# FNet mixing and a squared-ReLU layer on one core: the first tile's table on ScalarE's queue, and P's products ahead of Q's in the first front

## The chip, the core and the metric

The kernel runs on one core of a Trainium2 chip. The metric is the device time in microseconds (us) of one execution; less is better. Before the change the median of three runs is 1860.83 us, and the three lie between 1860.78 and 1861.01. One execution was also profiled; it took 1860.65 us, and its span, from the first instruction to the last, is 1858.6 us. The other 2.05 us lie outside the span.

The core's engines each work through their own instructions in order: TensorE (PE) multiplies matrices, VectorE (DVE), ScalarE (ACT) and GpSimd (POOL) work elementwise, SyncE (SP) issues most transfers. An engine that meets an instruction whose semaphores are not yet there stops until they are. Transfers that SP issues run on one queue (q1 in the profile), those that ACT issues on another (q10), those of POOL on a third (q0).

## What is computed

```python
def _attn_ref(x):                       # x: (8, 3008, 256)
    X = np.fft.fft(x, axis=1)
    X = np.fft.fft(X, axis=2)
    return X.real.astype(np.float32)

def _moe_ref(x, w_in, w_out):           # x: (24064, 256), w_in: (256, 2048), w_out: (2048, 256)
    h = x @ w_in
    r = np.maximum(h, 0.0)
    g = r * r
    return (g @ w_out).astype(np.float32)
```

The real part of a two-dimensional Fourier transform of each of 8 batches, then a two-layer network with a squared ReLU on each of the 24064 rows. x is float32. The weights arrive as 64-bit floats; the kernel loads them as pairs of 32-bit words and makes float32 of them itself.

## The kernel before

**The whole.** The transform along the sequence is made by products with cosine and sine tables, after the 3008 rows have been folded by their symmetries into 7 tiles. For each batch this gives two panels, Pt (cosine part, called P) and Qt (sine part, called Q), each of 128 features by 1505 frequencies. The transform along the features is multiplied into w_in once: G1 and G2 are w_in times a cosine and a sine table. Then h is G1 with Pt plus or minus G2 with Qt, and from h the network goes on. A "front" is one step of this, for a block of 252 frequencies and a pair of chunks of 128 hidden features: products with P, products with Q, then DVE adds and subtracts them into g. Each batch has 6 blocks of 8 fronts. After a front come ReLU and square on ACT, sums on POOL, and the products with w_out in a bilinear scheme with few multiplications (lines 1063 to 1125).

**The head.** In the first 31 us, batch 0's tiles are loaded, folded and multiplied while the tables and the first raw weights arrive. This part is written out by hand from line 1320 on. The tiles are 0 and 1 (95 and 94 rows), TWO = 2 and TWO + 1 = 3 (96 and 92 rows), and ODD0 = 4, 5 and 6 (128, 128 and 120 rows). They are worked off in the order 0, 4, 1, 5, 2, 3, 6. For each:

- `load_x` issues one transfer for x, on SP's queue; `load_table` issues the transfers for the cosine table, one for each run of rows that lies together (three for tile 0, one for tile 4), on the queue it is given, SP's by default;
- `fold` adds and subtracts rows on DVE; its last result w goes to the products; two columns of w go to `lone` by ACT (line 577);
- `turn_table` makes the sine table from the cosine table on ACT (line 228). Tile 0's sine table is loaded instead, on POOL's queue;
- `products_of("P0 E0")` and the like put the products on PE (line 769): P with the cosine table, Q with the sine table, E with the cosine table and the single column.

`awake(n)` (line 252) puts n products of the identity matrix with itself on PE. Their results are never read. Before tile 0's products there are 24 of them, after them 7.

`round_win(j, raw)` gives the steps by which the raw 64-bit words of chunk pair j of w_in become float32. In the hand-written part these are `first` (pair 0) and `second` (pair 1): `[0]` begins on DVE (line 300), `[1]` is two steps on ACT (lines 305 and 310), `[2]` is on DVE (line 320), `[3]` is the sum on POOL (line 329). `first[0]` stands on DVE between the folds of tiles 1 and 5.

`join_4`, `join_2` and `lo` put together parts of Pt and Qt on DVE (lines 817 to 823, 811 to 813); "lo" writes the 252 columns that the first front needs. `keep` copies the odd part out of its PSUM bank on ACT (line 830). For P that bank belongs to the pool `psh`, which has two buffers; the fronts of the head take theirs from the same pool. `ends_of(0)` multiplies G2 with a single column on PE (line 383), and `keep_ends` copies its two columns into gE on DVE (line 387); DVE needs gE and the window ew when it splits a front (line 1026).

**The order after the head.** `ORDER` (line 1446) is a list of tokens, each of which issues a step to one engine. Those that matter here: `sp` multiplies to spread one row of Qt over all partitions (PE, line 995), `et` copies the result into the window ew (ACT, line 996); `f0a` and `f0b` are the products of the two halves of front 0 (PE, lines 1011 and 1013), `d0a` and `d0b` split them on DVE (lines 1026 to 1029); `TSj`, `Hj` are the DVE steps of weight pair j (lines 300, 320), `PUj`, `PLj`, `PWj` its ACT steps, `PRj` its POOL step; `pgDj`, `pgCj` multiply it with the sine and the cosine table (PE, line 351), `GDj`, `GCj` copy these into G2 and G1 (ACT, line 374).

**Semaphores of transfers.** The transfers that SP and ACT issue take their semaphores in turn from the same eight, in the order in which the transfers are placed in the program. A transfer that takes a semaphore for the second time waits, before it is issued, until the transfer that had it before has landed.

Of the kernel before, what the change touches and what calls it, by code (L numbers as in the profile page):

```python
# [9 lines left out]
F32 = mybir.dt.float32  # L10
# [5 lines left out]
P = 128  # L16
# [68 lines left out]
def kernel(  # L85
# [12 lines left out]
    nc = tc.nc  # L98
# [8 lines left out]
    CH = 256  # L107
# [13 lines left out]
    fp = ctx.enter_context(tc.tile_pool(name="fp", bufs=3))  # L121
# [4 lines left out]
    sp = ctx.enter_context(tc.tile_pool(name="sp", bufs=2))  # L126
# [5 lines left out]
    psh = ctx.enter_context(tc.tile_pool(name="psh", bufs=2, space=PSUM))  # L132
# [13 lines left out]
    TWO = ODD0 - 2  # L146
# [14 lines left out]
    def later_rows(t):  # L161

        if t >= ODD0:
            return [(p, S // 8 + 1 + first, count, 1) for p, first, count in ODD[t - ODD0]]
        c, r0, step, rows = TILES[t]
        if t == TWO + 1:
            return [(p, TILES[TWO][1] + step * (2 * HALF2 - p - R), R, step) for p in range(0, ROWS2, R)]
        return [(0, r0, rows, step)]

    def load_x(b, t):  # L170
        if b and (t >= ODD0 or t == TWO + 1):
            xt[b, t] = xp.tile([P, 4, D], F32, name="xt", tag="x")
            for p, first, count, step in later_rows(t):
                nc.sync.dma_start(out=xt[b, t][p:p + count], in_=x[b, first:first + step * (count - 1) + 1:step])
            return
        c, r0, step, rows = TILES[t]

        while rows % 15 and rows % 16 and r0 + step * rows < NROW:
            rows += 1

        pool, tag = (gp, "g") if b == 0 and t < NT - NX else (xp, "x")
        xt[b, t] = pool.tile([P, 4, D], F32, name="xt", tag=tag)
        nc.sync.dma_start(out=xt[b, t][0:rows], in_=x[b, r0:r0 + step * (rows - 1) + 1:step])
# [4 lines left out]
    def load_later(i):  # L188
        if i < len(LATER):
            load_x(*LATER[i])  # L190
# [3 lines left out]
    cosT, sinT = ([const.tile([P, 2, WT], F32, name=nm), sp.tile([P, 2, WL], F32, name=nm + "l", tag="s")]  # L194
                  for nm in ("cosT", "sinT"))

    def part_of(tab, t):
        return tab[t in LATE]
# [4 lines left out]
    G1 = const.tile([P, F], F32, name="G1")  # L203
# [4 lines left out]
    def load_table(tab, src, tiles, queue=nc.sync):  # L208

        for t in tiles:  # L210
            c, r0, step, rows = TILES[t]
            for i, (s0, count) in enumerate(row_tiles(S)):
                mine = [r for r in range(count) if (s0 + r - r0) % step == 0 and 0 <= (s0 + r - r0) // step < rows]
                if mine:
                    o, m = (s0 + mine[0] - r0) // step, len(mine)
                    while m % 15 and m % 16 and o + m < P and mine[0] + step * m < P:
                        m += 1
                    nk = NC[0][c]
                    queue.dma_start(out=part_of(tab, t)[o:o + m, :, PLACE[t]:PLACE[t] + nk],
                                    in_=src[mine[0]:mine[0] + step * (m - 1) + 1:step, :, i, 0:nk])  # L220
# [31 lines left out]
    def awake(n):  # L252
        filled = psh.tile([P, CH], F32, name="filled", tag="h")
        for _ in range(n):
            nc.tensor.matmul(filled[:, 0:P], ident, ident, start=True, stop=True)
# [123 lines left out]
    def ends_of(j):  # L379
        ps = psd.tile([P, CH], F32, name="pe", tag="d")  # L380
        for h in range(2):
            fc = j + NJ * h
            nc.tensor.matmul(ps[:, h:h + 1], G2[:, fc * P:(fc + 1) * P], last, start=True, stop=True)
        return ps

    def keep_ends(j, ps):
        nc.vector.tensor_copy(gE[:, j::NJ], ps[:, 0:2])

    def take_ends(j):
        nc.sync.dma_start(out=gE[:, j::NJ], in_=g_dram[j].rearrange("(h f) -> f h", h=2))  # L390
# [612 lines left out]
    def store_upper():  # L1003
        nc.sync.dma_start(out=e_dram[0:1, KH:NKT], in_=PQE[0][1][P - 1:P, KH:NKT])

    def front_half(b, k0, n, j, h):

        pt, qt = PQE[b]
        ks, fs = slice(k0, k0 + n), slice((j + NJ * h) * P, (j + NJ * h + 1) * P)
        ps = psh.tile([P, 2, CH], F32, name="ph", tag="h")  # L1010
        nc.tensor.matmul(ps[:, 0, 0:n], G1[:, fs], pt[:, ks], start=True, stop=True)
        rows = P if b else P - 1
        nc.tensor.matmul(ps[:, 1, 0:n], G2[0:rows, fs], qt[0:rows, ks], start=True, stop=True)  # L1013
        return ps
# [291 lines left out]
    def p_part(*names):  # L1306
        for nm in names:
            for kp in range(2):
                groups[0, kp, nm]()

    def q_part(*names):
        for nm in names:
            for kp in range(2):
                groups[1, kp, nm]()
# [3 lines left out]
            (p_part if nm[0] == "P" else q_part)({"P": "", "Q": "", "E": "e"}[nm[0]] + nm[1:])  # L1318

    start()  # L1320
    awake(24)
    load_x(0, 0)
    load_table(cosT, cos_s, (0,))
    load_x(0, ODD0)
    load_x(0, 1)
    nc.scalar.copy(turn[0:1, 0, 0:1], ident[0:1, 0:1])
    nc.gpsimd.tensor_copy(turn[0:1, 0, 1:2], xt[0, 0][0:1, 0, 0:1])
    load_table(sinT, sin_s, (0,), nc.gpsimd)
    load_table(cosT, cos_s, (1, TWO, TWO + 1), nc.gpsimd)
    load_table(cosT, cos_s, (ODD0,))  # L1330
    load_x(0, ODD0 + 1)
    raw = {("in", 0): load(pair_in(0))}
# [2 lines left out]
    for dst, src in ((cosd, cos_d), (sind[:, :, 0:P - 1], sin_d)):  # L1335
        nc.sync.dma_start(out=dst, in_=src.rearrange("(c p) m -> p c m", p=P))
    load_x(0, TWO + 1)
    load_x(0, ODD0 + 2)
    load_table(cosT, cos_s, (ODD0 + 2,))
    first = round_win(0, raw["in", 0])  # L1340
# [34 lines left out]
    sc = fold(ODD0 + 2, 1)  # L1375
    fold_beside(ODD0 + 2, sc)
    products_of("P6 E6")
    ends = ends_of(0)
    p_part("join_2")
    q_part("join_4")  # L1380
    products_of("Q6")
    second = round_win(1, raw["in", 1])
    second[0]()
    second[1]()
    p_part("lo", "keep")
    q_part("join_2")
    keep_ends(0, ends)
    q_part("lo")
    BLOCKS = [(k0, min(CK, NKT + 1 - k0)) for k0 in range(0, NKT, CK)]
    assert all(n % 3 == 0 for _, n in BLOCKS)  # L1390
    steps = [(b, k0, n, j) for b in range(B) for k0, n in BLOCKS for j in range(NJ)]
# [44 lines left out]
    def piece_beside():  # L1436
# [7 lines left out]
    ROUNDED = ['3', 'w0', '4', 'w1', '5', 'w2', '6', 'w3', '7', 'w4', 'w5', 'w6', 'w7']  # L1444
    PHASES = ('TS', 'PW', 'H', 'PR', 'PU', 'PL')
    ORDER = (
        'sp H1 PR1 TS2 PU2 TS3 f0a et PL2 f0b PW3 d0a H2 PR2 pgD1 d0b pgC1 GD1 TSw0 GC1 lc4 H3 PR3 rl0 PWw0 fe1 f1b gE1 pgC2 f1a '
        'd1b pgD2 GC2 d1a GD2 keep f2b TS4 fe2 rl1 pgD3 Hw0 gE2 GD3 dE3 pgC3 sq0 PRw0 d2b f2a GC3 TSw1 PW4 d2a f3b sq1 '
        'PWw1 H4 bk0 PR4 TS5 Hw1 rl2 PRw1 PW5 pgD4 f3a GD4 dE4 d3b pgC4 TSw2 d3a sq2 bk1 GC4 H5 PWw2 PR5 TS6 Hw2 '
        'PW6 PRw2 rl3 TSw3 H6 PWw3 pgD5 PR6 f4b GD5 dE5 f4a d4b sq3 pgC5 d4a bk2 GC5 rl4 TS7 Hw3 PW7 PRw3 TSw4 H7 lc1 '  # L1450
# [56 lines left out]
    def step(token):  # L1507


        what, nm = re.fullmatch("([A-Za-z]+?)(w?[0-9]*[ab]?)", token).groups()  # L1510
        if what in PHASES:
            rounds[nm][PHASES.index(what)]()
            if what == "H":
                freed.add(nm)
                load_more()
        elif what == "sp":
            made["et"] = spread_e()
        elif what == "et":
            made["et"]()
        elif what == "df":  # L1520
            for f in beginning:
                f()
        elif what == "lc":
            load_columns(int(nm or 4))
        elif what == "xl":
            for k in range(NX):
                load_later(k)
        elif what == "keep":
            q_part("keep")
        elif what == "restQ":  # L1530
            q_part("rest")
        elif what == "restP":
            p_part("rest")
        elif what == "spl":
            store_lower()
            load_window(0, *BLOCKS[1])
        elif what in ("pgC", "pgD"):
            made[what, nm] = dft_win(int(nm), int(what == "pgD"))
        elif what in ("GC", "GD"):
            keep_win(int(nm), int(what == "GD"), made["pg" + what[1], nm])  # L1540
        elif what == "fe":
            made["fe", nm] = ends_of(int(nm))
        elif what == "gE":
            keep_ends(int(nm), made["fe", nm])
        elif what == "dE":
            take_ends(int(nm))
        elif what in "fd":
            i, h = int(nm[:-1]), int(nm[-1] == "b")
            if what == "f":
                if i >= NJ and ("x", i) not in made:  # L1550
                    made["x", i] = True
                    load_columns(4)
                made[token] = front_half(*steps[i], h)
            else:
                split_half(*steps[i], h, front_at(i)[-1], made["f" + nm])
        elif what in ("rl", "sq"):
            (relu if what == "rl" else square)(steps[int(nm)][2], made["g", int(nm)])
        elif what == "cm":
            sums_of(int(nm))
        elif what in ("sc", "su"):  # L1560
            (copy_wout if what == "sc" else sum_wout)(int(nm[0]), int(nm[1] == "b"))
        elif what == "hi":
            rows_at(int(nm))
        else:
            assert what == "bk"
            back_at(int(nm))
# [20 lines left out]
    for i in range(PLAIN, len(steps) + 2):  # L1587
        if i < len(steps):
            b, k0, n, j = steps[i]
# [130 lines left out]
```

## Time and profile before

| | |
|---|---|
| median of three runs | 1860.83 us (1860.78 to 1861.01) |
| the profiled execution | 1860.65 us |
| its span | 1858.6 us |
| PE, idle in the first 100 us | 2.58 us |
| DVE, busy from 15 to 30 us | 14.83 of 15 us |
| the 16 DMA engines, busy from 5 to 30 us | 1.01 to 1.10 of each 5 us, as the profile counts it |

In a row of the timeline the first number is the start and the second the duration, both in us from the span's start; then come engine, line, operation, what is written and read, shapes and how many instructions the row stands for. In square brackets stands how long the engine had been idle and who ended it. PE shows two records for one float32 product. A row of the stages view gives a stretch, its length and for each engine the busy time and the number of instructions; PEclk is the share of the TensorE clock that was granted, and the last two numbers are the share of the DMA engines and GB/s.

### The profile page before, as it was taken

What the parts mean: (1) busy time and instruction counts of PE and PEld (TensorE: products, weight loads), DVE (VectorE), ACT (ScalarE), POOL (GpSimd) and SP (SyncE); (2) the same over time, 40 slices, a digit from 0 to 9 for tenths busy, and PEclk for the clock granted to TensorE, in tenths of its full rate; (3) what the DMA queues carried; (4) which work ended last, traced back from release to release, by engine and by line L of the source; (5) the groups of instructions that cost most, each with busy time, mean ns of one, the idle gap of its engine ahead of it and who ended that gap; (6) DMA issues with size and microseconds to landing.
All of it is one profiled execution on the core that took longest, in us unless ns stands there. A gap on an engine that the chain in (4) does not pass through costs nothing.

```text
span 1858.6 us, 33954 instructions
## 1 busy us (share of the span) xinstructions
PE 1850.1 (100%) x11360; PEld 1748.1 (94%) x11360; DVE 1474.3 (79%) x3472; ACT 1075.2 (58%) x1594; POOL 1461.2 (79%) x2137
## 2 busy tenths in 40 slices
PE   9999999999999999999999999999999999999999
PEld 7699999999999999999999999999999999999998
DVE  8998878887788878778788787788878887757666
ACT  5776546565555655656456564565645666444454
POOL 4499778788788887888778887788877878787885
PEclk9999999999999999999999999999999999999999
DMA  7441101111111101111011100111001100000010
GB/s 211 109 61 41 21 21 51 41 29 23 29 34 45 26 22 32 33 46 30 15 32 46 49 15 15 46 46 35 15 21 44 37 15 21 17 21 15 21 43 23
DMA packets 153265, 69.51 MB, mean 37 GB/s; under 512 B 132577, under 2 KB 144325, under 8 KB 153092
## 3 DMA queue, kind: packets, MB, share of 16 engines
q1 hardware_dynamic: 152546, 66.80, 14.6%
q8 instruction: 91, 1.49, 0.3%
q14 instruction: 82, 0.67, 0.1%
q0 software_dynamic: 416, 0.43, 0.1%
q10 hardware_dynamic: 130, 0.12, 0.0%
HBM read 42.60 MB, written 24.69 MB: 36 GB/s over the span
## 4 chain that ended last, share of the span: by engine, by line
PE 94%; DVE 2%; POOL 1%; ACT 1%; issue 0%; DMA 0%; SPq 0%; POOLq 0%; DVEq 0%; ACTq 0%
PE F L1105 34%; PE S L1105 23%; PE hQ L1040 17%; PE hP L1040 17%; PE pd L893 1%; PE pd L867 1%; PE pd L769 1%; PE pg L351 0%; PE fin L1214 0%; DVE fd L320 0%; DVE he L1026 0%; DVE wsum L420 0%; DVE g L1029 0%; ACT g L1053 0%; PE ph L1013 0%
## 5 line engine op out<-in xcount | busy, mean ns | idle before, releaser
L1053 ACT ACTIVATE g<-g 128x1008 f32<-128x1008 f32 (+1 forms) x384 | 399.4, 1040 | 307.3 <-DVE g L1049 282.1
L1044 DVE SCALAR_TENSOR_TENSOR he<-ew,gE,hP 128x252 f32<-128x252 f32 (+1 forms) x748 | 321.2, 471 | 284.1 <-PE hP L1040 284.1
L1056 ACT ACTIVATE g<-g 128x1008 f32<-128x1008 f32 (+1 forms) x384 | 399.4, 1040 | 12.0
L1040 PE MATMUL hQ<-Qt,G 128*128 128x252 f32 (+3 forms) x1496 | 379.3, 376 | 0.6 <-ACT g L1053 0.5
L1040 PE MATMUL hP<-Pt,G 128*128 128x252 f32 (+1 forms) x1496 | 378.9, 376 | 0.0
L1105 PE MATMUL F<-s,wsum 128*128 128x168 f32 (+1 forms) x1496 | 335.5, 306 | 0.0
L1040 PEld LDWEIGHTS hQ<-Qt,G 128*128 128x128 f32 (+1 forms) x1496 | 281.6, 190 | 38.5 <-issue 2.6
L1105 PE MATMUL F<-g,wout 128*128 128x168 f32 (+1 forms) x1496 | 304.2, 305 | 0.0
L1078 POOL TENSOR_TENSOR s<-g 128x168 f32<-128x168 f32 (+1 forms) x187 | 100.8, 539 | 254.3 <-ACT g L1056 132.7
L1048 DVE TENSOR_TENSOR g<-he,hQ 128x504 f32<-128x504 f32 (+1 forms) x374 | 252.9, 676 | 41.7 <-DVE he L1044 2.7
L1040 PEld LDWEIGHTS hP<-Pt,G 128*128 128x128 f32 x1496 | 265.9, 190 | 18.8 <-issue 0.7
L1105 PE MATMUL S<-s,wout 128*128 128x168 f32 (+1 forms) x1496 | 280.7, 306 | 0.8 <-POOL s L1085 0.8
L1105 PE MATMUL S<-s,wsum 128*128 128x168 f32 (+1 forms) x1496 | 273.6, 305 | 0.0
L1105 PE MATMUL F<-g,wsum 128*128 128x168 f32 (+1 forms) x1496 | 273.6, 305 | 0.0
L1049 DVE TENSOR_TENSOR g<-he,hQ 128x504 f32<-128x504 f32 (+1 forms) x374 | 250.7, 670 | 0.0
L1105 PEld LDWEIGHTS F<-s,wsum 128*128 128x128 f32 x1496 | 247.6, 190 | 0.0
L1105 PEld LDWEIGHTS S<-s,wsum 128*128 128x128 f32 x1496 | 239.2, 190 | 8.2 <-issue 0.2
L1105 PEld LDWEIGHTS F<-g,wsum 128*128 128x128 f32 x1496 | 239.3, 190 | 8.1
L1105 PEld LDWEIGHTS F<-g,wout 128*128 128x128 f32 x1496 | 239.3, 190 | 0.0
L1105 PEld LDWEIGHTS S<-s,wout 128*128 128x128 f32 x1496 | 231.0, 190 | 1.7 <-POOL s L1085 1.0
L1081 POOL TENSOR_TENSOR s<-s 128x336 f32<-128x336 f32 (+1 forms) x187 | 168.4, 901 | 14.7
L1084 POOL TENSOR_TENSOR s<-s 128x336 f32<-128x336 f32 (+1 forms) x187 | 167.6, 896 | 14.7
(226 smaller groups left out, 2479.0 us busy)
## 6 DMA issues: line engine op xcount, KB each, us to landing
out_dram<-os SPq DMA_DIRECT2D x376, 56.0 KB
xt<-in_x_dram SPq DMA_DIRECT2D x39, 384.0 KB
xt<-in_x_dram SPq DMA_DIRECT2D x63, 128.0 KB
raw<-in_moe_w_out_dram SPq DMA_DIRECT2D x20, 256.0 KB
ew<-e_dram SPq DMA_DIRECT2D x39, 126.0 KB
out_dram<-os SPq DMA_DIRECT2D x288, 7.0 KB
raw<-in_moe_w_in_dram SPq DMA_DIRECT2D x16, 256.0 KB
xt<-in_x_dram SPq DMA_DIRECT2D x2, 512.0 KB
```

Of the source, the lines that this page charges most:

```text
L769: nc.tensor.matmul(ps[0:w.shape[-1]], w, part_of(cosT if lone_e else tab, t)[0:rows, kp, PLACE[t]:PLACE[t] + NC[kp][c]], start=t == ts[0] ...
L867: nc.tensor.matmul(to, left(pair[part != which]), columns(tab, TWO, o)[0:HALF2], start=True, stop=True)
L1040: nc.tensor.matmul(to[:, h, 0:n], w[:, fs], v[:, ks], start=h == 0, stop=True, skip_group_check=True)
L1044: nc.vector.scalar_tensor_tensor(out=t[:, h, 0:n], in0=window[b, k0][:, 0:n], scalar=gE[:, fc:fc + 1], in1=hP[:, h, 0:n], op0=ALU.mult, op ...
L1048: tt(out=g[:, :, 0:n], in0=t[:, :, 0:n], in1=hQ[:, :, 0:n], op=ALU.add)
L1049: tt(out=g[:, :, n:2 * n][:, :, ::-1], in0=t[:, :, 0:n], in1=hQ[:, :, 0:n], op=ALU.subtract)
L1053: act(g[:, :, 0:2 * n], g[:, :, 0:2 * n], AF.Relu)
L1056: act(g[:, :, 0:2 * n], g[:, :, 0:2 * n], AF.Square)
L1078: gt(out=s[:, 11], in0=b2[:, 0], in1=b1[:, 0], op=SUB)
L1081: gt(out=s[:, 4:6], in0=s[:, 4:6], in1=s[:, 10:11].to_broadcast([P, 2, tb]), op=SUB)
L1084: gt(out=s[:, 6:9:2], in0=s[:, 2:4], in1=s[:, 6:8], op=ADD)
L1105: nc.tensor.matmul(acc[nm][:, slot, 0:tb], w, v, start=q == 0 and nm not in begun, stop=q == end - 1, skip_group_check=True)
```

## The change

The first table's three transfers go to ACT's queue, behind a small copy on ACT; the two transfers each for the tables of tiles 2 and 3 go from POOL's queue to SP's, between x tile 3 and x tile 6. Five of the 24 idle products ahead of tile 0 go. `front_half` can make its product with P alone; the token `fp` asks for that, and the later `f` for the same half then makes only the product with Q. The products `fp0a` and `fp0b` stand first in the order, then the ends of pair 0 (`fe0`, formerly ahead of Q6), then Q's products with `sp` between them. On DVE the copy of the ends (`gE0`) goes from ahead of Q's "lo" to behind H1, and `TS3` goes behind `d0a`. In the hand-written part P's "lo" and "keep" go ahead of `second[1]`.

```diff
-    def front_half(b, k0, n, j, h):
+    beginning_of = {}
+
+    def front_half(b, k0, n, j, h, only_p=False):
 
         pt, qt = PQE[b]
         ks, fs = slice(k0, k0 + n), slice((j + NJ * h) * P, (j + NJ * h + 1) * P)
-        ps = psh.tile([P, 2, CH], F32, name="ph", tag="h")
-        nc.tensor.matmul(ps[:, 0, 0:n], G1[:, fs], pt[:, ks], start=True, stop=True)
+        ps = beginning_of.pop((k0, j, h), None)
+        if ps is None:
+            ps = psh.tile([P, 2, CH], F32, name="ph", tag="h")
+            nc.tensor.matmul(ps[:, 0, 0:n], G1[:, fs], pt[:, ks], start=True, stop=True)
+        if only_p:
+            beginning_of[k0, j, h] = ps
+            return
...
     start()
-    awake(24)
+    awake(19)
     load_x(0, 0)
-    load_table(cosT, cos_s, (0,))
     load_x(0, ODD0)
     load_x(0, 1)
     nc.scalar.copy(turn[0:1, 0, 0:1], ident[0:1, 0:1])
+    load_table(cosT, cos_s, (0,), nc.scalar)
     nc.gpsimd.tensor_copy(turn[0:1, 0, 1:2], xt[0, 0][0:1, 0, 0:1])
     load_table(sinT, sin_s, (0,), nc.gpsimd)
-    load_table(cosT, cos_s, (1, TWO, TWO + 1), nc.gpsimd)
+    load_table(cosT, cos_s, (1,), nc.gpsimd)
     load_table(cosT, cos_s, (ODD0,))
...
     load_x(0, TWO + 1)
+    load_table(cosT, cos_s, (TWO, TWO + 1))
     load_x(0, ODD0 + 2)
...
     products_of("P6 E6")
-    ends = ends_of(0)
     p_part("join_2")
     q_part("join_4")
     products_of("Q6")
     second = round_win(1, raw["in", 1])
     second[0]()
+    p_part("lo", "keep")
     second[1]()
-    p_part("lo", "keep")
-    q_part("join_2")
-    keep_ends(0, ends)
-    q_part("lo")
+    q_part("join_2", "lo")
...
-        'sp H1 PR1 TS2 PU2 TS3 f0a et PL2 f0b PW3 d0a H2 PR2 pgD1 ...
+        'fp0a fp0b fe0 f0a sp H1 PR1 gE0 f0b et TS2 PU2 d0a TS3 PL2 PW3 H2 PR2 pgD1 ...
...
+        elif what == "fp":
+            front_half(*steps[int(nm[:-1])], int(nm[-1] == "b"), True)
```

In the program built from the changed kernel the eight semaphores fall out thus: x of tile 0 has the first, x of tile 4 the second, x of tile 1 the third, then the table of tile 4, x of tile 5 and the two halves of raw pair 0 the next four. The first of the three transfers on ACT's queue has the eighth. The second of them has the second again and waits for x of tile 4; the third has the third again and waits for x of tile 1. PE's first product of tile 0 waits for all three.

## The prediction

> **What bounds the kernel now.** I read the shares of the page first, then TensorE's timeline of the head, then who ended its pauses.
>
> ```profile
> PE 1850.1 (100%) x11360; PEld 1748.1 (94%) x11360; DVE 1474.3 (79%) x3472; ACT 1075.2 (58%) x1594; POOL 1461.2 (79%) x2137
> 1.37 6.98 PE L255 MATMUL filled<-ident 128*128 128x128 f32 x48 [1.37 <-POOL ident masks.py:199]
> 8.19 0.58 PE L769 MATMUL pd<-cosT,w 95*128 95x95 f32 x4
> 9.05 1.75 PE L255 MATMUL filled<-ident 128*128 128x128 f32 x14
> ...
> 15.75 0.61 PE L769 MATMUL pd<-sinT,w 94*127 94x95 f32 x4
> 16.99 1.53 PE L769 MATMUL pd<-cosTl,w 128*128 128x377 f32 x4 [0.63 <-DVE w L576]
> ...
> 29.04 0.50 PE L383 MATMUL pe<-ident,G 128*128 128x1 f32 x4
> 29.41 1.51 PE L769 MATMUL pd<-sinTl,w 120*127 120x377 f32 x4
> 31.36 0.69 PE L995 MATMUL pe<-Qt,ident 128*128 128x252 f32 x2 [0.44 <-DVE Qt L748]
> ```
>
> PE is busy for all but 8.5 us of the span. A change in the head can win only what PE idles there or does for nothing: 1.37 us at the start, 0.63 us ahead of tile 5, 0.44 us ahead of the first front, and idle products. From 31.36 to 50 us the chain of waits runs on PE almost without a break, so what PE is late at 31 us it is late at the end; I found no slack behind it that takes a shift up.
>
> **What the change does to the head.** Five idle products go. The stages show their price and the clock:
>
> ```profile
> 1.30:4.20 2.90, 2.83 (x13) 1.00 0.70 177
> 4.30:8.10 3.80, 3.80 (x36) 1.00 0.95 259
> 1854.00:1856.00 2.00, 0.44 (x2) 1.00 0.38 125
> 1856.00:1858.60 2.60, 0.00 (x0) 0.82 0.29 97
> ```
>
> Up to 4.2 us a record takes 2.90/13 = 0.22 us, later 3.80/36 = 0.106 us: PE begins at half speed. Two records are one product, so five cost 1.1 us, and PE is through with its 19 at about 8.19 - 1.1 = 7.1 us. Tile 0's fold is done by then: its w row starts at 6.40 us and takes 0.76. What isn't there is the table. Before, SP issued its three transfers at 1.20 to 2.55 us, behind x of tile 0 alone, and PE did not wait for them at 8.19. Now the second is issued only when x of tile 4 has landed, the third when x of tile 1 has. These rows tell when that was:
>
> ```profile
> 4.41 0.69 DVE L567 TENSOR_TENSOR fs<-xt 95x512 f32<-95x512 f32 x1 [2.44 <-DMA xt<-in_x_dram]
> 7.65 0.69 DVE L567 TENSOR_TENSOR fs<-xt 128x512 f32<-128x512 f32 x1 [0.48 <-DMA xt<-in_x_dram]
> 8.99 0.50 SPq L1336 DMA_DIRECT2D sind<-in_sin_d_dram  x1
> 9.85 1.11 ACT L228 ACTIVATE sinT<-cosT,sind 128x377 f32<-128x377 f32 x2 [2.38 <-DMA cosT<-in_cos_s_dram]
> 14.17 0.43 DVE L300 TENSOR_SCALAR fd<-raw 128x512 uint32<-128x512 uint32 x1 [1.09 <-DMA cosTl<-in_cos_s_dram]
> SPq L183 <- DMA xt<-in_x_dram: 1.7, 1, 1.7
> ```
>
> x of tile 0 is there at 4.4, of tile 4 at 7.6, and of tile 1 at 9.0: SP's transfer of sind takes the semaphore that x of tile 1 had, and starts at 8.99, after a pause. (The last row shows SP itself held 1.7 us by such a wait.) With three small transfers fewer ahead of them the two x tiles are issued 1.4 us sooner, at 1.20 and 1.66. The DMA engines, only 54% busy in the first 5 us and full afterwards, bind too, so I take 1.2 of the 1.4: x of tile 1 lands at 7.8 us. Then ACT issues the third transfer. How long that takes to land no row shows for this queue. From below: a transfer to g_dram on otherwise free engines, 1.18 us on the chain. From above: 6.4 us, the median of the same 24 KB on POOL's queue among the same traffic.
>
> ```profile
> 64.99 1.18 DMA g_dram<-G
> sinT<-in_sin_s_dram POOLq DMA_DIRECT2D x3, 23.8 KB, 6.4
> ```
>
> I take 2.2 us, near the lower end, because on SP's queue x of tile 0, 16 times the bytes, needs only 3.66 us from its issue at 0.75 to its fold: 1.2 us, plus about 1 us because the DMA engines are full. So tile 0's products start at 10.0 us and not at 8.19; bounds 9.0 to 14.2. ACT stands still meanwhile, from 2.2 to 8.3 us; behind the wait stands the copy of tile 0's single columns (7.26 before), which E0 needs, and it still comes ahead of the table. `turn_table` of tile 4 waits for a table that lands at 9.85 or sooner, so it loses nothing.
>
> From there PE's list is as before. P0 to Q1 take 8.02 us (8.19 to the end of the last record's turn at 16.2), so tile 5 starts at 18.0, not 16.99. The raw weights do come sooner: they are issued 1.35 us sooner and lift DVE's pause of 1.09 us ahead of 14.17, and with it PE's 0.63 us; but PE is not yet there to use it. Tile 5 to E6 is 12.05 us (16.99 to 29.04), Q6 1.51 us: Q6 ends at 31.6 instead of 30.92, **+0.7 us**. (The ends' 0.37 us now come behind Q6.) The tables of tiles 2 and 3 on SP's queue cost nothing here: 290 KB that POOL's queue moved before through the same engines, needed by ACT at 21.8 and 22.6; SP issues them behind x of tile 3, which waits until raw pair 0 has landed, near 13 us. Should they be late, products of tiles 2 and 3 pay it one to one; I leave up to 0.5 us for this. x of tile 6, now behind them, lands no later, as the bytes ahead of it are the same. SP waits longer for semaphores (x of tile 2 now for tile 4's table), with four or more transfers still in the engines, so these stay full. POOL's queue loses four issues of 0.55 us; its next work is at 18.03.
>
> **The first front.** PE had waited 0.44 us for Q's "lo". Now two products with P (0.43 us each) and the ends (0.37) fill that, so the wait goes. PE's bank for them is freed by "keep", now ahead of ACT's steps for pair 1, some 2 us before it is needed. Counted from the end of Q6, PE reaches pgD1 at 4 x 0.43 + 0.53 + 0.37 = 2.6 us, before at 33.60 - 30.92 = 2.7. So far a gain of 0.1. But DVE gets new waits:
>
> ```profile
> 33.60 0.46 DVE L1026 SCALAR_TENSOR_TENSOR he<-ew,gE,ph 128x252 f32<-128x252 f32 x1
> 34.76 0.68 DVE L320 SCALAR_TENSOR_TENSOR fd<-raw,fd 128x512 uint32<-128x512 uint32 x1
> 35.62 1.27 POOL L329 TENSOR_TENSOR win<-fd,m 128x512 int32<-128x512 int32 x1 [2.22 <-PE pg L351]
> 36.94 1.13 PE L351 MATMUL pg<-win,cosd 128*128 128x256 f32 x4
> ```
>
> Before, H2 starts at 3.84 us after Q6, POOL's PR2 follows it, and pgC2 starts 50 ns after PR2's end, at +6.02: it has no slack. After: H1 ends at +1.0, the copy gE0 waits for the ends on PE until +1.35, TS2 ends near +2.4, d0a waits for the window (spread on PE until +2.3, copied by ACT in 0.35) until +2.7 and takes 1.16, then come TS3 (0.36) and H2 at +4.2. That is 0.36 later, so pgC2 comes at +6.4, where PE waits 0.75 us: **+0.3 us** against before. Bounds: 0, if TS2 runs without POOL's contention and the window comes sooner, and 0.8.
>
> **Sum.** +0.7 + 0.3 = +1.0 us on the profiled 1860.65, 1861.65. That execution stands 0.18 below the median, so I predict **1861.8 us**.
>
> **The rivals.** *The clock falls.* PE now idles from 7.1 to 10.0 us. In the tail its last product ends at 1854.66, and the mean clock of 0.82 over the last 2.6 us means half speed from 1857.7 on: 3.0 us without products, or a stretch that was 11% busy, sufficed. At the start about 2.9 us of products were needed to get out of it. If the pause of 2.9 us lies so in the clock's windows that one is judged idle, 3.4 us of the following products run at half speed: +1.7, time 1863.5. For it: the length, almost that of the tail; against it: a little under 3.0, and products at its rim. The Trainium skill, "TensorE: Matmul & The Clock Gate", Part 1, says that activity is judged in free-running windows of about 3.4 us and that one idle window halves the clock; by that rule the pause is just too short to fill a window, and the sum stays 1861.8 unless partly busy windows count as idle. The tail's 11% agrees that they may.
>
> *The table is no brake.* If x of tile 1 lands so soon, or the small transfer so fast, that tile 0 starts by 7.5 us, PE gains the 1.1 us of idle products; tile 5 then waits for DVE alone, which comes about 0.9 us sooner by the raw weights. Q6 ends another 0.4 sooner because the ends have left its way, and pgC2 gives 0.4 back: -0.9, time 1859.9. Against it: full DMA engines, and two landings in a row. That raw weights come sooner as promised is true in this case too; only here does it pay.
>
> *The third transfer is slow,* slower than the forecast by a full measure: it shares the engines as POOL's did, and lands midway to or at the upper bound, at 12 to 14.2 us. This is 2 to 4.2 us more, and a pause of 5 us or more brings the half clock for certain: 1861.8 + 2.1 + 1.7 = 1865.6, at most 1867.7. It decides the sign of the measurement from a start of about 11 us on, with the clock lost. For it: POOL's 6.4 us; against it: SP's queue, with 384 KB in 3.66 us.
>
> **How the numbers follow.** The forecast 0.42, the fallen clock 0.32, no brake 0.12, the slow transfer 0.12, the rest 0.02. A difference of 0.2% (3.7 us) is about what a measurement tells from no change. Faster by that much would need more than PE's whole idle time in the head: 0.02. Slower by it: the slow transfer and the upper edge of the fallen clock (start at 10.8 or later), 0.17. Within it 0.81. The range runs from 1859.6 (no brake) to 1865.0 (clock lost, start half a us late, 0.5 for late tables).
>
> **What would show it.** In the profile after: a pause of PE ahead of its first L769 row of 2 to 4 us, ended by a transfer of cosT; ACT's transfers of cosT starting where x of tiles 4 and 1 land; no pause of PE ahead of tile 5 and ahead of the first front; a new one of about 0.7 us ahead of the second pair of pg products, ended by POOL; and records of 0.21 us instead of 0.11 among the second idle products if the clock fell. A first L769 row at 7.1 to 7.5 us would refute the forecast.

## The result, and the profile after

| | before | after |
|---|---|---|
| median of five runs each, on one chip | 1861.01 us (1860.78 to 1863.35) | 1868.62 us (1868.26 to 1869.32) |
| span of the profiled execution | 1858.6 us | 1866.9 us |
| first product of tile 0 | 8.19 us | 13.18 us |
| first product of tile 5 | 16.99 us | 24.54 us |
| first product with w_out (tile mA) | 44.90 us | 53.11 us |

The ratio is 1.0039, with a 95% interval from 1.0028 to 1.005: slower by 7.6 us, where +1.0 was forecast. The time lies above the predicted range.

The last three rows divide the loss. Ahead of tile 0 it is 13.18 - 8.19 = 5.0 us. From there to tile 5 it grows by 24.54 - 16.99 - 5.0 = 2.6, and from tile 5 to mA by 53.11 - 44.90 - 7.55 = 0.7. That makes 8.2 at mA, and the span is 8.3 longer: nothing behind the head takes it up.

The timeline of TensorE in the changed kernel, in the form of the rows shown of before (start, duration, engine, line, operation, tiles, shapes, count, and in brackets the pause ahead and who is said to have ended it):

```profile
1.36 6.85 PE L255 MATMUL filled<-ident 128*128 128x128 f32 x38 [1.36 <-POOL ident masks.py:199]
13.18 1.14 PE L769 MATMUL pd<-cosT,w 95*128 95x95 f32 x4 [4.97 <-DVE fd L300]
14.97 3.25 PE L255 MATMUL filled<-ident 128*128 128x128 f32 x14
18.01 2.40 PE L769 MATMUL pd<-cosT,w 128*128 128x377 f32 x4
...
24.54 1.46 PE L769 MATMUL pd<-cosTl,w 128*128 128x377 f32 x4
...
37.78 1.01 PE L1015 MATMUL ph<-Pt,G 128*128 128x252 f32 x4
...
43.85 0.61 PE L383 MATMUL pe<-ident,G 128*128 128x1 f32 x4 [1.44 <-ACT G L374]
```

Three things are to be seen. PE pauses 4.97 us ahead of tile 0. The row names DVE's rounding step (L300), but that reads and writes weights, which tile 0's products do not touch; it merely ended close by. What they do wait for is the table, and its third transfer landed at 12.93. Then the products run at half speed: the 14 records of identity products take 3.25 us where they took 1.75 before, and tile 4's first row takes 2.40 instead of 1.43. The pauses ahead of tile 5 and ahead of the first front are gone, but there is a new one of 1.44 us ahead of the single columns of pair 1 (L383).

The stages of the same execution show the clock (stretch, length, PE's busy time and instructions, granted clock, share of the DMA engines, GB/s):

```profile
8.20:13.10 4.90, 0.01 (x1) 1.00 1.10 346
13.10:16.50 3.40, 3.32 (x15) 0.50 1.06 254
16.50:20.00 3.50, 3.50 (x13) 0.51 1.04 225
20.00:24.00 4.00, 4.00 (x22) 1.00 1.09 282
```

The trace has the clock halved from 13.13 to 19.96 us, 6.83 us. The engines that move data are full throughout (a share of 1.04 to 1.10).

ScalarE's timeline of the head shows the issues (ACTq is the queue's issuing):

```profile
1.35 0.38 ACTq L219 DMA_DIRECT2D cosT<-in_cos_s_dram  x1
2.03 0.19 ACT L1332 COPY turn<-ident 1x1 f32<-1x1 f32 x1
6.42 1.67 ACTq L219 DMA_DIRECT2D cosT<-in_cos_s_dram  x2
```

The first transfer goes out ahead of the small copy, though it stands behind it in the kernel's text. By the trace's semaphore events, x of tile 4 landed at 6.40 and x of tile 1 at 7.75; the second transfer went out at 6.42 and the third at 7.78. The three took 5.25, 5.32 and 5.16 us from issue to landing. The transfers that SP issued next took as long: x of tile 2 (384 KB, issued at 8.74) 6.36 us, cosd and sind (128 KB each) 5.41 and 4.95. By the packet records the third table transfer waited 3.8 us for its first packet (11.57), and all its packets were through by 12.20: the time went by ahead of the transfer, not in it.

VectorE shows what became of the weights that come sooner:

```profile
12.59 0.42 DVE L300 TENSOR_SCALAR fd<-raw 128x512 uint32<-128x512 uint32 x1
23.89 0.25 DVE L817 TENSOR_TENSOR db<-da,pd 128x95 f32<-128x95 f32 x1 [7.62 <-ACT da L788]
```

The first rounding step starts at 12.59 instead of 14.17, and from 16.27 on DVE idles for 7.62 us, because it waits for ACT's copy (da) of what PE has not yet made.

### The profile page after: what moved, and what is told of

Same layout as the page of the kernel before. It is cut to its first block, busy times and chain, and to the rows that moved or that the text cites. A ratio compares the mean times of both kernels' runs of the same rounds, so it can differ in the third digit from the quotient of the medians.

```text
span 1866.9 us, 33933 instructions
## 1 busy us (share of the span) xinstructions
PE 1852.9 (99%) x11350; PEld 1750.8 (94%) x11350; DVE 1472.4 (79%) x3472; ACT 1074.9 (58%) x1594; POOL 1458.6 (78%) x2133
## 4 chain that ended last, share of the span: by engine, by line
PE 95%; DVE 2%; POOL 1%; ACT 1%; issue 0%; DMA 0%; SPq 0%; DVEq 0%; POOLq 0%; ACTq 0%
PE F L1112 33%; PE S L1112 23%; PE hQ L1047 17%; PE hP L1047 17%; PE pd L769 2%; PE pd L893 1%; PE pd L867 1%; DVE fd L320 0%; DVE he L1033 0%; PE fin L1221 0%; DVE g L1036 0%; PE pg L351 0%; DVE wsum L420 0%; DVE g L1035 0%; DMA xt<-in_x_dram 0%
```

## The experiments

All have in common that the "kernel before" ran beside them on the same chip; its median was 1861.0 us in both batches that were timed (25 and 32 runs). "The front stretch" below is the time from tile 5's first product to the first with w_out (tile mA): 27.91 us before, 28.57 after.

**The first table back on SP's queue, all else as changed.**

```diff
     load_x(0, 0)
+    load_table(cosT, cos_s, (0,))
     load_x(0, ODD0)
...
-    load_table(cosT, cos_s, (0,), nc.scalar)
```

> The changed kernel with the first table's three transfers back on SP's queue, right behind x of tile 0; all else as changed. Theory (late table, then the half clock, make about 7 of the 8.3 us; the new order of the first front makes the other 1.3): no pause of PE ahead of tile 0's products above 0.3 us, no half clock after 8 us, tile 5 starts near 17.0 us as before, Q6 ends 0.4 us sooner than before, the first front costs 1.3 us: 1861.9 us. Rival (the new order of the first front and of the ends is what costs, and the pause at the start would be caught up by the sooner weights): 1866 us or more.

Measured 1861.65 us (1860.79 to 1862.88), ratio 1.0003 [0.9994, 1.0013]. Tile 0 starts at 8.16 without a pause, tile 5 at 16.71. So nearly all of the loss hangs on the queue and the place of this one table.

**The table's queue alone, in the kernel before.** The same two lines, the other way round, with 24 idle products and the old order.

> The kernel before with one edit: the first table's three transfers on ACT's queue, placed as in the change (24 idle products, all else as before). Theory: the third transfer is issued when x of tile 1 lands (7.8 us) and lands near 13 us, PE pauses 4 to 5 us, Q6 ends 4 us later than before with the full clock and 7 us later if the clock is halved: 1865 to 1868 us. Rival (order of the first front): within 1 us of the kernel before.

Measured 1867.75 us (1867.1 to 1868.89), ratio 1.0038 [1.0023, 1.0053].

```profile
1.37 7.22 PE L255 MATMUL filled<-ident 128*128 128x128 f32 x48 [1.37 <-POOL ident masks.py:199]
13.82 1.14 PE L769 MATMUL pd<-cosT,w 95*128 95x95 f32 x4 [5.23 <-DMA cosT<-in_cos_s_dram]
15.60 3.09 PE L255 MATMUL filled<-ident 128*128 128x128 f32 x14
```

In this timeline of PE the releaser is named as it is, the transfer of cosT, and the clock falls with all 24 idle products too: it is halved from 11.56 to 18.39. The one edit brings 6.75 us, where the whole change brings 7.6.

**The same queue without the waits.** The load is placed ahead of x of tile 0 in the program, where it takes semaphores that nothing had before it.

```diff
     awake(19)
+    load_table(cosT, cos_s, (0,), nc.scalar)
     load_x(0, 0)
...
-    load_table(cosT, cos_s, (0,), nc.scalar)
```

> The changed kernel with the three transfers still on ACT's queue, but placed ahead of all x tiles in the program, so that none of them waits for a semaphore of an x tile. Theory that the two waits make the table late (each transfer lands some 5.2 us after its issue, as the first one did, issues at 0.7 to 2.3 us): table there at 6 to 7.5 us, PE's pause ahead of tile 0 below 0.5 us, raw pair 0 and tile 5's fold about 1 us sooner than before, Q6 1.3 us sooner, less 1.3 us in the first front: 1860.8 us. Rival that ACT's queue is slow whatever it waits for, since SP's transfers fill the engines: table after 9 us, a pause of 2 us or more, 1863 us or more.

Measured 1861.0 us (1860.39 to 1862.65), ratio 1.0002 [0.9992, 1.0011]. ACT issues all three between 0.75 and 2.13 us; they land at 4.86, 6.19 and 8.03, and PE starts tile 0 at 8.16, after 0.74 us of waiting for the last of them. The place alone is worth 7.6 us (1868.62 against 1861.0): what cost the time is not that ACT issues the table but that two of its transfers wait, before their issue, for x tiles to land. With no wait the transfers still take 4.1, 5.0 and 6.3 us.

**Is the transfer slow because of its queue, or because the engines are full?** Two kernels hold SP back by a small transfer that reads a fold's result. In the first, ACT issues its transfers behind the fold of tile 0:

```diff
-    load_table(cosT, cos_s, (0,), nc.scalar)
...
     load_table(cosT, cos_s, (1,), nc.gpsimd)
+    fold(0)
+    load_table(cosT, cos_s, (0,), nc.scalar)
+    fold(ODD0)
+    held = dp.tile([1, 128], F32, name="held")
+    nc.sync.dma_start(out=held, in_=folded[0, ODD0][0:1, 0, 0:128])
     load_table(cosT, cos_s, (ODD0,))
...
-    fold(0)
...
-    fold(ODD0)
```

> The changed kernel, with the first table's three transfers placed behind the fold of tile 0 on ACT's queue (issued from about 7.3 to 8.5 us, none of them waiting for a semaphore of another transfer), and with SP's queue held from x of tile 1 to the end of tile 4's fold (about 8.5 us) by a small transfer that reads this fold's result: SP's transfers that stood in the engines in the changed kernel are not issued yet when the table's are. Theory (a small transfer on ACT's queue is slow because the engines are full of what SP issued before it): with the engines nearly empty each of the three lands 1.5 to 2.5 us after its issue, and the products of tile 0 start near 10.5 us. Rival (transfers on ACT's queue take about 5 us in themselves): each lands 4.5 to 5.5 us after its issue, as in the changed kernel, and tile 0 starts at 13 us or later. The time of the whole says nothing here, since everything that SP loads comes later.

Issued at 7.31, 7.74 and 8.22, the three landed 1.86, 1.84 and 1.82 us later. POOL's queue became faster with them. The issues in the first 14 us (transfer, queue, count, size, median us from issue to landing), first of the changed kernel, then of this one:

```profile
sinT<-in_sin_s_dram POOLq DMA_DIRECT2D x3, 23.8 KB, 5.4
cosT<-in_cos_s_dram POOLq DMA_DIRECT2D x2, 23.8 KB, 5.2
```

```profile
sinT<-in_sin_s_dram POOLq DMA_DIRECT2D x3, 23.8 KB, 2.9
cosT<-in_cos_s_dram POOLq DMA_DIRECT2D x2, 23.8 KB, 2.1
```

The same 24 KB on the same queues take about two to three times as long when SP has filled the engines (busy for 1.02 to 1.06 of each us from 7 to 10 us in the changed kernel, for 0.27 to 0.44 here). The rival, a slow queue, is refuted. The third table transfer waited 1.1 us for its first packet here and 3.8 there, and its packets took 0.3 and 0.6 us, so most of the difference lies ahead of the first packet. Whether it waits there at the engines or on the way to them is not told apart: holding SP back empties both. In the second kernel SP is held only until the fold of tile 0, and the table stands where the change put it:

```diff
     load_table(cosT, cos_s, (1,), nc.gpsimd)
+    fold(0)
+    held = dp.tile([1, 128], F32, name="held")
+    nc.sync.dma_start(out=held, in_=folded[0, 0][0:1, 0, 0:128])
     load_table(cosT, cos_s, (ODD0,))
...
-    fold(0)
```

> The changed kernel, with SP's queue held from x of tile 1 to the end of tile 0's fold (about 7.2 us) by a small transfer that reads this fold's result. The table's three transfers stand where the change put them, issued at 1.4 to 2.3 us without waiting for another transfer, and share the engines with x of tiles 0, 4 and 1 and POOL's transfers alone. Theory (engines full): they land somewhat sooner after their issue than the 4.1, 5.0 and 6.3 us that they took with no wait but with all of SP's queue beside them, the third above all: 4 to 5.5 us, since x of tile 4 and tile 1 are still ahead of it. Rival (ACT's queue slow in itself): about 5 us for each, all alike. The time of the whole says nothing here.

Here the three took 5.23, 6.12 and 5.83 us, longer than the 4 to 5.5 expected: the three x tiles, 1.25 MB, are enough to fill the engines until about 6.6 us, and no table landed before. It tells nothing apart by itself, though POOL's transfers, issued from 5.33 us on, took 2.7 and 2.1 us in it, much as in the first. The two kernels took 1866.84 and 1862.19 us in one run each.

**What is the half clock worth?** The changed kernel with 41 idle products instead of 19, which keep PE busy until the table is there.

```diff
-    awake(19)
+    awake(41)
```

> The changed kernel with 41 instead of 19 idle products ahead of tile 0, so that PE is busy until 12 or 13 us while the table is on its way. Theory (the half clock from 13.1 to 20.0 us cost 3.4 us of the 8.3, because PE had paused for 5 us): table still at 13 us, tile 0's products at 13.2 us, full clock, tile 5 near 21.2 us instead of 24.5, 1865.2 us. Rival (the half clock is hidden, since DVE or the transfers bound the head anyway): 1868.5 us.

Measured 1865.99 us (1864.87 to 1870.47), ratio 1.003 [1.002, 1.0039]. The pause is 0.49 us, tile 0 starts at 13.33 at the full clock, and tile 5 at 21.41. That is 8.08 us for tile 0 to tile 5, where the changed kernel takes 11.36: the half clock costs 3.3 us there, 2.6 by the medians of the two kernels.

**The order of the first front alone.** The loads and idle products of before, the new order.

```diff
-    awake(19)
+    awake(24)
     load_x(0, 0)
+    load_table(cosT, cos_s, (0,))
...
-    load_table(cosT, cos_s, (0,), nc.scalar)
...
-    load_table(cosT, cos_s, (1,), nc.gpsimd)
+    load_table(cosT, cos_s, (1, TWO, TWO + 1), nc.gpsimd)
...
-    load_table(cosT, cos_s, (TWO, TWO + 1))
```

> The kernel before with only the new order of the first front, of the ends and of P's lo and keep; tables, queues and the 24 idle products as before. Theory: PE up to Q6 as before but for the ends (0.4 us sooner), no pause ahead of the first front, then a pause of 1.2 to 1.5 us behind pgC1, because ACT copies G behind a step of pair 3 that waits for TS3 on DVE, now behind d0a: 1861.7 us. Rival (this order is the main cost): 1866 us or more; second rival (the pause in the changed kernel came from the shifted transfers, not from the order): 1860.2 us.

Measured 1862.07 us (1861.11 to 1863.29), ratio 1.0006 [0.9997, 1.0016]: not told from no change by the time, but its front stretch is 28.64 us, 0.73 more than before, and the 1.44 us pause at L383 is there as in the changed kernel.

**The loads alone, without the waits,** in the order of before: 19 idle products, the first table on ACT's queue ahead of x of tile 0, the tables of tiles 2 and 3 on SP's queue.

```diff
-    awake(24)
+    awake(19)
+    load_table(cosT, cos_s, (0,), nc.scalar)
     load_x(0, 0)
-    load_table(cosT, cos_s, (0,))
...
-    load_table(cosT, cos_s, (1, TWO, TWO + 1), nc.gpsimd)
+    load_table(cosT, cos_s, (1,), nc.gpsimd)
...
+    load_table(cosT, cos_s, (TWO, TWO + 1))
```

> The kernel before with the loads of the change alone, the table's transfers placed first as in e2: 19 idle products, tables of tiles 2 and 3 on SP, the order of the first front as before. Theory: tile 0's products near 8.2 us (the table lands at 8.0), tile 5 0.7 us sooner than before thanks to the sooner raw weights, the wait of 0.44 us for Q's lo stays: 1860.1 us. Rival (what is won in the head is lost again behind it, since DVE and the transfers set the pace there): 1860.9 us.

Measured 1859.95 us (1859.48 to 1860.49), ratio 0.9994 [0.9985, 1.0002], not told from no change. Tile 5 starts at 16.18 instead of 16.99 with no pause ahead of it; the front stretch is 27.93, as before.

**Why PE pauses 1.44 us in the first front.** What the row of L383 waits for is ACT's copy of G (L374). ACT's and DVE's timelines of the changed kernel just ahead of it:

```profile
42.18 0.71 ACT L305 ACTIVATE raw<-raw 128x512 f32<-128x512 f32 x1 [0.17 <-DVE fd L300]
42.75 0.78 ACT L310 ACTIVATE m<-raw,ramp 128x512 uint32<-128x512 uint32 x1
43.39 0.67 ACT L374 ACTIVATE G<-pg 128x256 f32<-128x256 f32 x2
```

```profile
39.17 0.16 DVE L387 COPY gE<-pe 128x2 f32<-128x2 f32 x1 [0.22 <-PE pe L383]
39.25 1.39 DVE L300 TENSOR_SCALAR fd<-raw 128x512 uint32<-128x512 uint32 x1
...
41.73 0.42 DVE L300 TENSOR_SCALAR fd<-raw 128x512 uint32<-128x512 uint32 x1
```

The copies of G stand behind pair 3's two steps in ACT's order; these wait for TS3 (41.73 on DVE), which the change put behind d0a. And TS2, which the change put behind gE0's wait, now runs beside POOL's sum for pair 1 (PR1, 39.09 to 40.36) and takes 1.39 us. The kernel before had a slow step as well, as its row shows:

```profile
31.84 1.84 DVE L300 TENSOR_SCALAR fd<-raw 128x512 uint32<-128x512 uint32 x2
```

There TS2 took 0.42 us, mostly ahead of PR1, and TS3 1.50 beside it; ACT began pair 2's steps 0.4 us after the end of H1, in the changed kernel 1.7 us after it. In all twelve profiled kernels the step that runs beside PR1 takes 1.39 to 1.50 us. Two kernels mend the one or both, each with the table's load ahead of x of tile 0. First TS3 alone:

```diff
-        'fp0a fp0b fe0 f0a sp H1 PR1 gE0 f0b et TS2 PU2 d0a TS3 PL2 PW3 H2 PR2 pgD1 ...
+        'fp0a fp0b fe0 f0a sp H1 PR1 gE0 f0b et TS2 PU2 TS3 d0a PL2 PW3 H2 PR2 pgD1 ...
```

> The variant with the table's transfers placed first (e2), with TS3 back ahead of d0a on DVE. Theory (ACT copies G late because pair 3's step waits for TS3): the pause of 1.44 us behind pgC1 falls to 0.8 us or less, 0.7 us less time than e2: 1860.3 us. Rival (the pause is made by the copy gE0, which waits for the ends, and by TS2 beside POOL): 1.2 us or more remain, 1861.0 us.

Measured 1860.46 us (1860.02 to 1861.13), ratio 0.9997 [0.9988, 1.0006], not told from no change. The pause fell only to 1.12 us, between what theory and rival gave: TS3 is a part of it, and the smaller one. Then both steps ahead of gE0, and ACT's PW3 ahead of d0a (which changes the order of neither engine):

```diff
-        'fp0a fp0b fe0 f0a sp H1 PR1 gE0 f0b et TS2 PU2 d0a TS3 PL2 PW3 H2 PR2 pgD1 ...
+        'fp0a fp0b fe0 f0a sp H1 PR1 TS2 PU2 TS3 gE0 f0b et PL2 PW3 d0a H2 PR2 pgD1 ...
```

> As e2, with DVE's and ACT's steps in the order of before behind H1 (TS2, PU2, TS3 ahead, then gE0, window, PL2, PW3, d0a); P's products and the ends still ahead of Q's. Theory: G is copied as soon as PE has made it, the pause behind pgC1 is 0.5 us or less, and both gains of the head stay: 1859.7 us. Rival: as for e7, 1861.0 us.

Measured 1859.59 us (1859.23 to 1859.99), ratio 0.9991 [0.9982, 1.0]; it is the fastest of all kernels here, 1.4 us below the kernel before, though the interval just touches 1. PE's timeline:

```profile
7.72 0.66 PE L769 MATMUL pd<-cosT,w 95*128 95x95 f32 x4
15.80 1.46 PE L769 MATMUL pd<-cosTl,w 128*128 128x377 f32 x4
34.25 0.61 PE L383 MATMUL pe<-ident,G 128*128 128x1 f32 x4 [0.25 <-ACT G L374]
```

Tile 0 starts 0.47 us sooner than before, tile 5 1.19 sooner, and the pause is down to 0.25. So the larger part of the pause came from TS2 behind gE0. But the front stretch is 27.93 us, as long as before: what this kernel wins lies ahead of tile 5, and P's products ahead of Q's win nothing even in the best of the three orders run here.

## Why the prediction was wrong

**The step that failed** is "I take 2.2 us, near the lower end", the time of the table's third transfer from issue to landing. Measured: 5.16 us. The steps on the table that lead to it held: the two waits are there, x of tile 1 landed at 7.75 (forecast 7.8), and the third transfer went out at 7.78. Tile 0 so started at 13.2 us, not 10.0, inside the bounds of 9.0 to 14.2, and what came is the rival "the third transfer is slow" (start at 12 to 14.2, clock lost), to which I gave 0.12. For this start that rival's price is 1861.8 + 3.2 + 1.7 = 1866.7, still 1.9 us short: the half clock lasted twice as long as I had priced it, and the first front lost 0.7 us.

The row that should have decided was the 6.4 us of POOL's queue: the same size at the same time among the same traffic. I chose the row of SP's x of tile 0 because a larger transfer was faster there, but that one was the first of all and met empty engines. The lower row, 1.18 us for g_dram, I misread too: it moves 1 KB, and the engines were not free beside it, but busy for 0.73 of its time. The quiet kernel beside the changed one shows both sides: 1.8 us on mostly idle engines, close to my 2.2, and 5.2 on full ones. The 1 us that I added for full engines was a guess at a backlog that costs about 3.3 us (5.16 against 1.82 to 1.86). The Trainium skill, "DMA: Bandwidth & Descriptors", section "Issuing engines are not separate DMA queues", says that transfers of all issuing engines run on the same 16 engines and interleave. The trace agrees as far as a transfer on another queue is no way round the backlog (5.16 us beside SP's 5.41).

**The half clock** was a rival with the right mechanism and half its size: 1.7 us for one stretch of 3.4 us. It lasted 6.83 us, twice 3.413, and cost 2.6 to 3.3. The Trainium skill, "TensorE: Matmul & The Clock Gate", Part 1, gives free-running windows of about 3.4 us, half clock after an idle one and full clock after a busy one. The windows agree: in the kernel before, the clock rises at 4.247 and falls at 1857.684, 543 times 3.4133 us apart. So does the fall, at 13.13 after a window without products; but a wholly idle window is not needed, since in the kernel with the table's queue alone the clock fell at 11.56 after a window in which PE was busy for 0.43 us. The way back does not agree: the stretch from 13.1 to 16.5 is busy for 3.32 of 3.40 us, and the clock stays halved for a second one, though at the start of the kernel before 2.88 us of products were enough. Why it stayed halved is open.

**Five idle products** fewer were to end the rest at 7.1 us, 1.1 sooner. This failed as well, without effect, since the table came later still: the clock rose at 6.30 us in the profiled execution and at 4.25 before, so the 19 end at 8.21, only 0.14 us sooner than the 24 did (8.35).

**The head without the table** came out as forecast: no pause ahead of tile 5, none ahead of the first front, no wait for the tables of tiles 2 and 3.

**The first front** was mis-sized and misplaced. I had +0.3, and with the ends moved behind Q6 (-0.37) about -0.1 from tile 5 on; measured +0.7. I followed the chain from H2 over POOL's PR2 to pgC2 and found 0.75 us of waiting there. What binds comes sooner and runs through ACT: TS2 and TS3 late, pair 3's two steps late behind them, the copies of G queued behind these, and with them the single columns of pair 1. I had named TS3's new place, but not what stands behind its successor on ACT. TS2 itself, which I had put at about 1 us, took 1.39.

**No slack behind the head** was right: 8.2 us late at mA, 8.3 at the end.

Summed with measured terms: +5.0 (start of tile 0), +3.3 (half clock), -0.7 (tile 0 to tile 5 takes 8.08 us at the full clock instead of 8.80, its pause being gone), +0.7 (from tile 5 on) = +8.3 on the spans; +7.6 by the medians. The profiled execution of the kernel before has the soonest rise of the clock of all that were profiled, which may be why the spans differ by more than the medians; no run shows it.

## What to carry to other kernels

Price a transfer by the traffic that was issued ahead of it, not by the queue it is issued on. Of several rows for such a transfer, the one taken in the same microseconds among the same traffic counts: here the row of 6.4 us, beside 5.16 measured and my estimate of 2.2. Where transfers take semaphores in turn, the place in the program decides what a small, urgent one waits for; moving the same load on the same queue to the front of the program took 7.6 us off. And when a step moves on one engine, follow its successor into the next engine's order and ask what stands behind it there.

## What the hardware showed that I had not expected

A pause of PE well under one window can halve the clock, and not always. A pause of 1.41 to 1.44 us at L383 is in seven of the profiled executions (the changed kernel and six experiments). In two of them, the table back on SP and the quiet kernel, the clock then fell for 3.41 us; in the five others it did not. The stages of the kernel with the table back on SP, PE alone:

```profile
34.00:37.20 3.20, 1.76 (x11) 1.00 0.33 2
37.30:40.60 3.30, 3.30 (x9) 0.50 0.51 158
```

Counted in windows of 3.413 us from the clock's first or last rise, PE was busy for 1.97 us (33.85 to 37.26) and, in the quiet kernel, 2.00 us (38.22 to 41.63) of the window ahead of the fall. In the changed kernel the pause (42.41 to 43.85) also lies within one window (40.44 to 43.85), PE was busy for 1.97 us of it as well, and the clock held. Nor does an early or late place tell them apart: the clock fell with the pause at 0.8 to 2.3 and 0.3 to 1.7 us of its window, and held with it at 2.0 to 3.4 us (the changed kernel) and at 0.0 to 1.4 us (SP held until tile 0's fold). What decides stays open.

When the clock first rises differs between executions of like kernels: between 4.25 us and 7.50 us in those profiled here, though the first idle product starts at 1.36 or 1.37 in each. Counted back from the rise in steps of 3.413 us, PE was busy for 2.88 us or more of the last window ahead of it in all twelve, and for 2.72 us or less of the one before. That fits a rise that comes at the end of the first such window that is busy enough, and then depends on where the first product falls in these windows. Idle products at the start are therefore not worth a fixed time.
